# A state-space scan and a gated FFN on one core: compact pair states, decays of the first two blocks from TensorE, a shorter weight conversion, every engine in written order

## The chip, the core and the metric

The kernel runs on one core of a Trainium2 chip. A core has five engines with queues of their own: TensorE (PE; PEld are its weight loads), VectorE (DVE), ScalarE (ACT), GpSimd (POOL) and SyncE (SP), which here issues every DMA. The metric is the device time of one execution in microseconds, the median of several runs, less is better.

## What is computed

The first half is a Mamba-2 scan. Inputs are x (4 batches, 8 heads, 768 steps, 32 channels), a (one decay per step), B and C (16 states per step), all fp32. The second half is an FFN over the 4 x 768 = 3072 tokens, each with 8 x 32 = 256 channels, with 1536 hidden channels. Its three weight matrices come as fp64, the rest as fp32.

```
# per batch and head, in chunks of the sequence
cum  = cumsum(log(clip(a, 1e-6, 1)))
L    = exp(cum[i] - cum[j]) for i >= j, else 0
y    = (C B^T * L) x  +  exp(cum) * (C state)
state= exp(sum log a) * state + sum_j exp(cum[-1] - cum[j]) B[j] x[j]
# then per token
xn   = y / sqrt(mean(y*y) + 1e-6) * rms_g
out  = (silu(xn @ w_gate) * (xn @ w_val)) @ w_out
```

The result does not depend on the length of a chunk, and the kernel takes 128 steps.

## The kernel before

**Tiling.** A batch has 6 chunks of 128 steps, the run 24 chunks, or 12 pairs. Two pairs are the 512 tokens of one of 6 blocks. `load(p)` (line 80) brings x, B and C of a pair, time on the partitions, so that B and C come in runs of 64 bytes and x in runs of 128. All DMAs go through SP's queue.

**Decays.** The opening turns a into logs with time on the partitions, and by products with triangular matrices into the three factors of line 219. For the triangle L it also makes the cumulated logs as rows (line 229) and writes them to DRAM; `spread(g)` (line 279) reads the 8 x 128 values of a chunk back to all 128 partitions (512 KB written to SBUF), `decays(g)` (286) makes eight ScalarE exponentials with a bias per head, and `causal` clears the upper half on POOL (247).

**Scan of a pair.** `scale` multiplies B and C with their factors. `turn` (265) transposes B, scaled C and C of a chunk on TensorE; two ScalarE copies and one masked VectorE product take the result out of PSUM. `products` (295) forms C B^T for pairs of heads on 32-row strips of the array, and VectorE multiplies with L. `step_state` (313) multiplies scaled B with x as one 128 x 256 product per chunk, of which a mask keeps the blocks of equal heads, and carries the state on. `outputs` (337) adds the carried-in part (`inter`) and the part inside the chunk (`intra`, one 32-column matmul per head), copies y to SBUF on ScalarE and squares it on POOL. Norm: `norm_sums` and `norm_apply`.

**Weights.** VectorE turns fp64 words into fp32 in eight steps per piece of 512 columns (`convert`, lines 138 to 155); there are 18 pieces, in a ring of four raw buffers.

**FFN of a block.** `gate_val(blk, f)` (417) is four fp32 matmuls of 512 columns in two passes each for one of 12 hidden slices f, then sigmoid on ScalarE and two VectorE products, u and h. `project` (431) makes the output of 128 tokens from all 12. They share five PSUM banks with the scan's products.

**Order.** The kernel is written in the order below, with the next block's scan laid between the gate steps; a planner may start an instruction earlier or later than it is written, where its tiles allow it. In each step of the loop the scan of block blk + 1 runs beside the FFN of block blk, and L of block blk + 2 is made in the projection.

```
    for steps in scan_steps(0):
        run(steps)
    norm_sums(0)
    weights(2)
    norm_apply(0)
    for g in range(4, 8):
        decays(g)
```

Of the kernel before, what the change touches and what calls it, by code (L numbers as in the profile page):

```python
# [10 lines left out]
I32 = mybir.dt.int32  # L11
AF = mybir.ActivationFunctionType
# [5 lines left out]
def kernel(  # L18
# [27 lines left out]

    nc = tc.nc
# [11 lines left out]
    TB = 512  # L59
    NBLK = T // TB  # L60

# [3 lines left out]
    cvt = ctx.enter_context(tc.tile_pool(name="cvt", bufs=1))  # L65
# [3 lines left out]
    dram = ctx.enter_context(tc.tile_pool(name="dram", bufs=1, space=bass.MemoryType.DRAM))  # L69

# [3 lines left out]

    a_sb = const.tile([BH, S], FP32, name="a_sb")
    nc.sync.dma_start(out=a_sb, in_=a.rearrange("b h s -> (b h) s"))

    st = {}

    def load(p):  # L80
        b, c0 = divmod(2 * p, NC)
        xr = raw.tile([P, 2, NH, D], FP32, tag="xr", name="xr")
        br = raw.tile([P, 2, NH, N], FP32, tag="br", name="br")
        cr = raw.tile([P, 2, NH, N], FP32, tag="cr", name="cr")
        for i in range(2):
            sl = slice((c0 + i) * P, (c0 + i + 1) * P)
            for dst, src in ((br, B), (cr, C), (xr, x)):
                nc.sync.dma_start(out=dst[:, i], in_=src[b, :, sl, :].rearrange("h s n -> s h n"))  # L88
        st[p] = {"x": xr, "B": br, "C": cr}

    load(0)
    load(1)

    load(2)
    load(3)

    gcol = const.tile([P, 2], FP32, name="gcol")
    gv_ = moe_rms_g.rearrange("(q t d) -> q d t", t=2, d=D)
    for q in range(NQ):
        nc.sync.dma_start(out=gcol[q * D:(q + 1) * D, :], in_=gv_[q])  # L100


    WC = 256
    NWC = DF // WC
# [4 lines left out]
    def words(w):  # L109
# [4 lines left out]
    wsrc = {"g": words(moe_w_gate).rearrange("(q t d) f -> q d t f", t=2, d=D),  # L114
            "v": words(moe_w_val).rearrange("(q t d) f -> q d t f", t=2, d=D),
            "o": words(moe_w_out).rearrange("(o i) m -> i o m", i=P)}
    wraw = {}

    def fetch(name, j):
        r = raw.tile([P, 2, 2 * WC], I32, tag="wr", name="wr")  # L120
        if name == "o":
            nc.sync.dma_start(out=r, in_=wsrc[name][:, 2 * j:2 * j + 2])
        else:
            for q in range(NQ):
                nc.sync.dma_start(out=r[q * D:(q + 1) * D],
                                  in_=wsrc[name][q][:, :, 2 * WC * j:2 * WC * (j + 1)])
        wraw[name, j] = r.rearrange("p t (f w) -> p t f w", w=2)

    def convert(name, j):


        r = wraw.pop((name, j))
        lo, hi = r[:, :, :, 0], r[:, :, :, 1]
        cs = slice(WC * j, WC * (j + 1))
        dst = {"g": wg[:, :, cs], "v": wv[:, :, cs], "o": wo[:, 2 * j:2 * j + 2]}[name]
        shape = [P, 2, WC]
        e = cvt.tile(shape, I32, tag="e", name="e")
        nc.vector.tensor_scalar(out=e, in0=hi, scalar1=20, scalar2=0x7FF,
                                op0=ALU.logical_shift_right, op1=ALU.bitwise_and)
        nc.vector.tensor_scalar(out=e, in0=e, scalar1=896.0, scalar2=1151.0,  # L140
                                op0=ALU.max, op1=ALU.min)
        nc.vector.tensor_scalar(out=e, in0=e, scalar1=-896.0, scalar2=2.0 ** 23,
                                op0=ALU.add, op1=ALU.mult)
        nc.vector.scalar_tensor_tensor(out=e, in0=hi, scalar=-2 ** 31, in1=e,  # L144
                                       op0=ALU.bitwise_and, op1=ALU.bitwise_or)
# [12 lines left out]
    pending = [(n, j) for j in range(NWC) for n in "gv"] + [("o", j) for j in range(NWC)]  # L158
    AHEAD = 3
    for n, j in pending[:AHEAD]:  # L160
        fetch(n, j)

    def weights(k):
        for _ in range(min(k, len(pending))):
            if len(pending) > AHEAD:
                fetch(*pending[AHEAD])
            convert(*pending.pop(0))


    ident = const.tile([P, P], FP32, name="ident")  # L170
    make_identity(nc, ident)
    ones = const.tile([P, P], FP32, name="ones")
    nc.vector.memset(ones, 1.0)
# [10 lines left out]
    mean1 = const.tile([P, 1], FP32, name="mean1")  # L184
    nc.vector.memset(mean1, 1.0 / DM)
# [339 lines left out]
```

## Time and profile before

| | |
|---|---|
| time, median of 3 runs | 535.24 us (534.09 to 536.27) |
| the profiled execution | 536.25 us, its span 534.5 us |
| TensorE busy | 481.3 us, 90% of the span |
| VectorE busy | 252.8 us, 47% |
| ScalarE busy | 159.7 us, 30% |
| POOL busy | 51.3 us, 10% |
| moved by DMA | 32.03 MB in 87868 packets |

The span is the time from the first to the last instruction in the trace; the device time holds a little more. A busy share is a mean over the span, and TensorE's 90% has stretches of half that in it, so the rows further down are read by stretch. PEclk is the granted TensorE clock, 1.00 for 2.4 GHz.

### The profile page before, as it was taken

The page shows a single profiled execution, that of the slowest core. Times are in us where ns is not written, and L with a number is a line of the kernel's source. Part 1 is how long each engine was busy: PE and PEld are TensorE (multiplying, and loading weights), DVE is VectorE, ACT ScalarE, POOL GpSimd, SP SyncE. Part 2 cuts the span into 40 slices and gives each one's busy share as a digit, 9 for nine tenths or more (in the row PEclk, how much of TensorE's full clock was granted, in tenths as well). Part 3 has the DMA queues.
Part 4 walks back from the last instruction along what each step waited for, and adds up shares of the span by engine and source line. Part 5 has one row for each costly group of instructions (what it writes and reads, how often), then busy time and mean ns, then how long its engine had stood idle before and what let it go on. Part 6 is the DMA issues. An engine that isn't in the chain of part 4 may idle for free.

```text
span 534.5 us, 5748 instructions
## 1 busy us (share of the span) xinstructions
PE 481.3 (90%) x2082; PEld 293.8 (55%) x2082; DVE 252.8 (47%) x503; ACT 159.7 (30%) x377; POOL 51.3 (10%) x53
## 2 busy tenths in 40 slices
PE   4519595878899999999999999999999999999997
PEld 3306343333587444785444784455864547844476
DVE  2484858877995535113645213555026561134410
ACT  3146578401454128502155303211011211011100
POOL 1013403000241001200001200000000001000000
PEclk9755697887979999999998999999999999999999
DMA  8899960222971023300250200000000000000000
GB/s 103 145 262 200 207 162 15 64 95 68 240 160 49 0 66 53 109 21 10 20 115 5 70 20 11 0 1 0 21 20 1 1 1 10 21 10 0 1 10 29
DMA packets 87868, 32.03 MB, mean 60 GB/s; under 512 B 76864, under 2 KB 80128, under 8 KB 87840
## 3 DMA queue, kind: packets, MB, share of 16 engines
q1 hardware_dynamic: 87840, 31.67, 25.9%
q8 instruction: 16, 0.26, 0.2%
q14 instruction: 12, 0.10, 0.1%
HBM read 28.41 MB, written 3.24 MB: 59 GB/s over the span
## 4 chain that ended last, share of the span: by engine, by line
PE 74%; DVE 6%; ACT 5%; DMA 5%; SPq 4%; issue 4%; POOL 1%; DVEq 0%; POOLq 0%; ACTq 0%
PE o L434 24%; PE val L422 21%; PE gate L422 21%; DMA L<-rows 3%; SPq L88 3%; PE g L302 2%; ACT L L291 2%; PE y L354 2%; PE y L344 1%; PE ms L391 1%; PE rb L406 1%; ACT L425 1%; ACT L291 1%; DVE e L144 1%; POOL L L247 1%
## 5 line engine op out<-in xcount | busy, mean ns | idle before, releaser
L422 PE MATMUL val<-xn,wv 128*128 128x512 f32 x288 | 140.4, 611 | 7.8 <-DVE wv L155 7.1
L422 PE MATMUL gate<-xn,wg 128*128 128x512 f32 x288 | 142.2, 617 | 0.9 <-DVE xn L409 0.9
L434 PE MATMUL o<-wo,h 128*128 128x256 f32 x576 | 130.6, 386 | 1.1 <-DVE h L429 1.1
L434 PEld LDWEIGHTS o<-wo,h 128*128 128x128 f32 x576 | 110.6, 194 | 18.5 <-issue 2.4
L427 DVE TENSOR_TENSOR u<-sg,gate 128x512 f32<-128x512 f32 x72 | 49.4, 686 | 118.9 <-ACT sg L425 118.8
L422 PEld LDWEIGHTS val<-xn,wv 128*128 128x128 f32 x288 | 55.7, 195 | 78.7 <-issue 65.8
L425 ACT ACTIVATE sg<-gate 128x512 f32<-128x512 f32 x72 | 43.0, 597 | 153.7 <-PE gate L422 150.8
L422 PEld LDWEIGHTS gate<-xn,wg 128*128 128x128 f32 x288 | 54.5, 198 | 58.2 <-issue 50.3
L291 ACT ACTIVATE L<-L,neg 128x128 f32<-128x128 f32 x192 | 58.3, 389 | 20.4 <-DMA L<-rows 20.3
L429 DVE TENSOR_TENSOR h<-u,val 128x512 f32<-128x512 f32 x72 | 49.4, 687 | 29.4 <-PE val L422 29.0
L437 ACT COPY ob<-o 128x256 f32<-128x256 f32 x24 | 8.9, 372 | 109.1 <-PE o L434 108.1
L378 POOL TENSOR_TENSOR sq<-yt 128x512 f32<-128x512 f32 x12 | 15.1, 1258 | 264.2 <-ACT yt L377 264.2
L247 POOL TENSOR_SCALAR_AFFINE_SELECT L<-L 128x1024 f32<-128x1024 f32 x24 | 28.0, 1168 | 112.4 <-ACT L L291 107.6
L309 DVE TENSOR_TENSOR L<-g,L 128x256 f32<-128x256 f32 x96 | 33.4, 417 | 6.0 <-PE g L302 3.2
L354 PE MATMUL y<-L,xr 128*32 128x128 f32 x384 | 17.9, 300 | 17.3 <-DVE L L309 17.3
L409 DVE SCALAR_TENSOR_TENSOR xn<-yt,gcol,rb 128x512 f32<-128x512 f32 x12 | 8.5, 744 | 39.1 <-PE rb L406 39.0
L354 PEld LDWEIGHTS y<-L,xr 128*32 128x32 f32 x384 | 11.8, 117 | 25.1 <-DVE L L309 19.5
L302 PE MATMUL g<-CT,BT 32*128 32x256 f32 x192 | 21.0, 470 | 3.2 <-DVE u L427 3.2
L302 PEld LDWEIGHTS g<-CT,BT 32*128 32x128 f32 x192 | 11.7, 214 | 14.9 <-issue 8.7
L377 ACT COPY yt<-y 128x512 f32<-128x512 f32 x12 | 7.0, 585 | 40.6 <-PE y L344 40.6
L271 ACT COPY BT<-tp 128x128 f32<-128x128 f32 x24 | 6.3, 263 | 39.8 <-PE tp L269 31.4
L320 PE MATMUL A_ps<-xr,Bd 128*128 128x256 f32 x40 | 12.9, 406 | 3.7 <-DMA xr<-in_x_dram 2.9
(72 smaller groups left out, 293.4 us busy)
## 6 DMA issues: line engine op xcount, KB each, us to landing
L<-rows SPq DMA_DIRECT2D x24, 512.0 KB, 5.7
xr<-in_x_dram SPq DMA_DIRECT2D x24, 128.0 KB, 3.4
wr<-in_moe_w_gate_dram SPq DMA_DIRECT2D x24, 128.0 KB, 3.8
wr<-in_moe_w_val_dram SPq DMA_DIRECT2D x24, 128.0 KB, 3.6
wr<-in_moe_w_out_dram SPq DMA_DIRECT2D x6, 512.0 KB, 3.6
out_dram<-ob SPq DMA_DIRECT2D x24, 128.0 KB, 1.7
br<-in_B_dram SPq DMA_DIRECT2D x24, 64.0 KB, 3.0
cr<-in_C_dram SPq DMA_DIRECT2D x24, 64.0 KB, 2.9
```

The source lines that it names most:

```text
L88: nc.sync.dma_start(out=dst[:, i], in_=src[b, :, sl, :].rearrange("h s n -> s h n"))
L247: nc.gpsimd.affine_select(out=out_, in_=in_, pattern=[[0, NH], [1, P]], compare_op=ALU.is_ge, fill=0.0, base=0, channel_multiplier=-1)
L291: nc.scalar.activation(out=L[:, h], in_=L[:, h], func=AF.Exp, bias=neg[:, c, k:k + 1])
L302: nc.tensor.matmul(out=g[q][:, i], lhsT=s["BT"][r, i], rhs=s["CT"][r, i], start=(i == 0), stop=True, tile_position=(32 * q, 0), skip_group ...
L309: nc.vector.tensor_tensor(out=L, in0=g[q][:, i], in1=L, op=ALU.mult)
L354: nc.tensor.matmul(out=y[32 * q:32 * q + 32, t, i], lhsT=s["x"][:, i, 2 * q + t], rhs=Ls[2 * p + i][:, 2 * q + t], start=not opened and i ...
L378: nc.gpsimd.tensor_tensor(out=sqs[blk][:, :, tk], in0=yts[blk][:, :, tk], in1=yts[blk][:, :, tk], op=ALU.mult)
L422: nc.tensor.matmul(out=dst, lhsT=w[:, t, fs], rhs=xns[blk][:, t], start=(t == 0), stop=(t == 1))
L425: nc.scalar.activation(out=sg, in_=g, func=AF.Sigmoid)
L427: nc.vector.tensor_tensor(out=u, in0=sg, in1=g, op=ALU.mult)
L429: nc.vector.tensor_tensor(out=h, in0=u, in1=v, op=ALU.mult)
L434: nc.tensor.matmul(out=o, lhsT=hs_[blk, f][:, k * P:(k + 1) * P], rhs=wo[:, f], start=(f == 0), stop=(f == NF - 1))
```

## The change

- *Written order.* The planner is switched off: every engine takes its instructions in the order of the program. SP does so too.
- *Triangle decays.* For the first two blocks (chunks 0 to 7) L no longer goes by DRAM. `spans(g)` spreads the logs of a chunk over 128 columns and clears them below the diagonal on POOL, `sums(g)` multiplies with a triangular matrix on TensorE (two PSUM banks per chunk) and takes the exponential of 512 columns at a time on ScalarE, `select(g)` clears the upper half. For chunks 8 to 23 the spread sums by DRAM stay; `spread` is issued in gate steps 8 and 11, `decays` and `select` in the projection.
- *Conversion.* Eight VectorE steps become five; two clamps become ScalarE `Relu` steps. A piece is begun in one call of `convert` and finished in the next. There are 11 pieces, seven of them 1024 columns wide, in a ring of three raw buffers, one DMA each.
- *Pair states.* The states keep only the blocks of equal heads: `states(p)` makes four matmuls of 64 columns per chunk on column strips of the array, and `inter` four matmuls on quarter arrays where two full ones were. C is loaded twice as halves of even and odd heads into buffers that hold zeros for the others, so that the masked product of `turn` goes; `turn` makes four transposes and one ScalarE copy of all. The pair's products with L are four VectorE steps of 512 columns where eight of 256 were.
- *Smaller things.* The norm's factors are spread by transposes (one pass) where matmuls with the identity took two. Fewer buffers: L for three pairs, 12 hidden tiles where there were 15, single yt and rsb.

```diff
-    cvt = ctx.enter_context(tc.tile_pool(name="cvt", bufs=1))
+    cvt = ctx.enter_context(tc.tile_pool(name="cvt", bufs=2))
...
+    ctx.enter_context(tc.manual_schedule())
...
+    for k in range(4):
+        crs.append(const.tile([P, 2, 2, NH, N], FP32, name="cr%d" % k))
+        nc.vector.memset(crs[k], 0.0)
...
+        cr = crs[p % 4]
...
+            nc.sync.dma_start(out=br[:, i], in_=B[b, :, sl, :].rearrange("h s n -> s h n"))
+            for t in range(2):
+                nc.sync.dma_start(out=cr[:, i, t, t::2],
+                                  in_=C[b, t::2, sl, :].rearrange("h s n -> s h n"))
...
+    pieces = [(n, c, w) for c, w in ((0, 256), (256, 512), (768, 512), (1280, 256)) for n in "gv"]
+    pieces += [("o", c, 4) for c in range(0, NF, 4)]
+    fetched, begun = [], []
...
+            r = raw.tile([P, shape[0], 2 * shape[1]], I32, tag="wr", name="wr", bufs=3)
+            nc.sync.dma_start(out=r, in_=src)
...
+        nc.vector.tensor_scalar(out=e, in0=hi, scalar1=0x7FF00000, scalar2=None,
+                                op0=ALU.bitwise_and)
+        ef = e.bitcast(FP32)
+        nc.scalar.activation(out=ef, in_=e, func=AF.Relu, scale=-8.0, bias=etop)
+        nc.scalar.activation(out=e, in_=ef, func=AF.Relu, scale=-1.0, bias=einf)
         m = cvt.tile(shape, I32, tag="m", name="m")
         nc.vector.tensor_scalar(out=m, in0=hi, scalar1=0xFFFFF, scalar2=0x100000,
                                 op0=ALU.bitwise_and, op1=ALU.bitwise_or)
-        l = cvt.tile(shape, I32, tag="l", name="l")
-        nc.vector.tensor_scalar(out=l, in0=lo, scalar1=8, scalar2=None,
-                                op0=ALU.logical_shift_right)
-        f = cvt.tile(shape, FP32, tag="f", name="f")
-        nc.vector.scalar_tensor_tensor(out=f, in0=l, scalar=2.0 ** -24, in1=m,
+        f = m.bitcast(FP32)
+        nc.vector.scalar_tensor_tensor(out=f, in0=lo.bitcast(U32), scalar=2.0 ** -32, in1=m,
                                        op0=ALU.mult, op1=ALU.add)
+        begun.append((hi, e, f, dst))
...
+    def finish():
+        hi, e, f, dst = begun.pop(0)
+        nc.vector.scalar_tensor_tensor(out=e, in0=hi, scalar=-2 ** 31, in1=e,
+                                       op0=ALU.bitwise_and, op1=ALU.bitwise_or)
         nc.vector.scalar_tensor_tensor(out=dst, in0=f, scalar=2.0 ** -20, in1=e.bitcast(FP32),
                                        op0=ALU.mult, op1=ALU.mult)
...
+    def convert():
+        if pieces:
+            fetch()
+        if fetched:
+            begin()
+        if len(begun) > 1 or (begun and not fetched):
+            finish()
...
+    load(0)
+    fetch(1)
+    load(1)
+    fetch(1)
+    gcol = const.tile([P, 2], FP32, name="gcol")
+    nc.sync.dma_start(out=gcol, in_=moe_rms_g.rearrange("(t p) -> p t", p=P))
+    fetch(2)
+    load(2)
+    load(3)
...
+    def spans(g):
+        b, c = divmod(g, NC)
+        lams[g] = ssd.tile([P, NH, P], FP32, tag="lam", name="lam")
+        causal(lams[g], la[:, c, b * NH:(b + 1) * NH].unsqueeze(2).to_broadcast([P, NH, P]))
+    def sums(g):
+        lam = lams.pop(g)
+        L = pair_tile(g)
+        for k in range(2):
+            hs = slice(4 * k, 4 * k + 4)
+            e = bank("e", (P, 4, P))
+            nc.tensor.matmul(out=e.rearrange("p h m -> p (h m)"), lhsT=after,
+                             rhs=lam[:, hs].rearrange("p h m -> p (h m)"),
+                             start=True, stop=True)
+            nc.scalar.activation(out=L[:, hs], in_=e, func=AF.Exp)
...
+    def select(g):
+        causal(pair_tile(g), pair_tile(g))
...
+        tp = mm.tile([P, 4, P], FP32, tag="tp", name="tp")
...
+        nc.scalar.copy(out=s["T"][:, i], in_=tp)
...
+            L = Ls[p][:, :, 2 * q:2 * q + 2].rearrange("p i t m -> p i (t m)")
+            nc.vector.tensor_tensor(out=L, in0=g[q], in1=L, op=ALU.mult)
...
+        A_ps = bank("A_ps", (P, 2, 2, D))
+        for i in range(n):
+            for q in range(NQ):
+                nc.tensor.matmul(
+                    out=A_ps[32 * q:32 * q + 32, i].rearrange("p t d -> p (t d)"),
+                    lhsT=s["Bd"][:, i, 2 * q:2 * q + 2].rearrange("p t n -> p (t n)"),
+                    rhs=s["x"][:, i, 2 * q:2 * q + 2].rearrange("p t d -> p (t d)"),
+                    start=(i == 0), stop=True, tile_position=(0, 32 * q),
+                    skip_group_check=True)
+        new = ssd.tile([P, 2, 2, D], FP32, tag="A", name="A")
+        nc.vector.tensor_tensor(
+            out=new[:, 0:n], in0=A_ps[:, 0:n],
+            in1=tmask.unsqueeze(1).unsqueeze(3).to_broadcast([P, n, 2, D]), op=ALU.mult)
...
+        y = mm.tile([P, 2, 512], FP32, tag="y", name="y")
...
+            S, CdT = state[2 * p + i - 1], s["T"][:, i, 1]
+            for q in range(NQ):
+                r = slice(32 * q, 32 * q + 32)
+                o = 64 * (q % 2)
                 nc.tensor.matmul(
-                    out=y[:, t, i],
-                    lhsT=state[2 * p + i - 1][:, t].rearrange("p q d -> p (q d)"),
-                    rhs=s["CdT"][:, i], start=not opened and i == 0 and t == 0, stop=True,
+                    out=y[o:o + 64, q // 2, i * P:(i + 1) * P],
+                    lhsT=S[r].rearrange("p t d -> p (t d)"), rhs=CdT[r],
+                    start=start, stop=True, tile_position=(32 * q, o),
...
-            nc.tensor.matmul(out=rb[:, k], lhsT=rsb[:, k], rhs=ident, start=True, stop=True)
+            nc.tensor.transpose(out=rb[:, k], in_=rsb[:, k], identity=ident)
...
+        hs_[blk, f] = h = ffn.tile([P, TB], FP32, tag="h", name="h", bufs=NF)
...
+    spans(0)
+    spans(1)
+    sums(0)
+    scale(0)
+    turn(0, 0)
+    turn(0, 1)
+    spans(2)
+    begin()
+    select(0)
+    sums(1)
...
+    spans(3)
+    select(1)
+    products(0)
+    states(0)
+    sums(2)
+    scale(1)
+    turn(1, 0)
+    turn(1, 1)
+    begin()
+    finish()
+    select(2)
+    sums(3)
+    outputs(0)
+    select(3)
+    products(1)
+    states(1)
+    convert()
+    spans(4)
+    spans(5)
+    outputs(1)
+    norm_sums(0)
+    sums(4)
+    convert()
+    norm_spread(0)
+    spans(6)
+    select(4)
+    sums(5)
+    norm_apply(0)
+    spans(7)
+    select(5)
+    sums(6)
+    select(6)
+    sums(7)
+    select(7)
...
+            [(states, p), (scale, q)],
...
-    for g in range(8):
-        spread(g)
-    for g in range(4):
-        decays(g)
...
             gate_val(blk, f)
+            if blk == 0:
+                convert()
             run(todo[f])
-            if blk == 0:
-                weights(2 if f % 2 == 0 and f < NF - 2 else 1)
-        for k in range(TB // P):
+            if blk + 2 < NBLK and f in (8, 11):
+                for g in range(4 * (blk + 2) + 2 * (f == 11), 4 * (blk + 2) + 2 * (f == 11) + 2):
+                    spread(g)
...
+                select(4 * (blk + 2) + k)
+            if blk + 1 < NBLK:
+                if k == 0:
+                    norm_sums(blk + 1)
+                if k == 1:
+                    norm_spread(blk + 1)
+                if k == 2:
+                    norm_apply(blk + 1)
```

## Rows read from the trace of the kernel before

**Rows 1.** stretches; columns: length, busy us (instructions) per engine, PEclk, DMA share, GB/s

```profile
0.00:63.60 63.60, 33.80 (x180) 22.75 (x180) 35.83 (x85) 27.34 (x83) 14.17 (x22) 0.68 0.89 179
63.60:146.80 83.20, 66.50 (x256) 32.79 (x256) 66.72 (x144) 34.36 (x76) 9.14 (x6) 0.85 0.43 114
146.80:170.00 23.20, 23.16 (x97) 19.93 (x98) 19.41 (x36) 10.62 (x35) 7.70 (x6) 0.87 0.52 115
170.00:243.00 73.00, 71.93 (x329) 43.95 (x328) 24.66 (x46) 27.43 (x58) 7.46 (x7) 1.00 0.20 47
243.00:321.60 78.60, 76.34 (x346) 46.80 (x345) 31.32 (x59) 26.48 (x56) 6.63 (x6) 0.98 0.20 41
321.60:469.35 147.75, 147.60 (x690) 91.47 (x689) 58.39 (x111) 24.41 (x53) 6.18 (x6) 1.00 0.02 8
469.35:534.50 65.15, 61.92 (x192) 36.13 (x191) 16.46 (x24) 9.03 (x17) 0.00 (x0) 1.00 0.03 10
```

**Rows 2.** chain of waits, opening; columns: start, us, what

```profile
63.56 3.78 PE gate L422 x4
```

**Rows 3.** timeline, opening; start, us, engine, line, operation, [idle before <-releaser]

```profile
7.07 0.33 ACT L217 ACTIVATE d_sb<-d_ps 128x192 f32<-128x192 f32 x1 [0.31 <-PE d_ps L214]
...
18.36 0.58 SPq L88 DMA_DIRECT2D xr<-in_x_dram  x1
...
34.00 9.46 ACT L291 ACTIVATE L<-L,neg 128x128 f32<-128x128 f32 x32 [12.47 <-DMA L<-rows]
```

**Rows 4.** DMA issues of the page; KB each, median us to landing

```profile
L<-rows SPq DMA_DIRECT2D x24, 512.0 KB, 5.7
...
wr<-in_moe_w_gate_dram SPq DMA_DIRECT2D x24, 128.0 KB, 3.8
```

**Rows 5.** timeline of VectorE, one quiet conversion piece

```profile
29.33 0.43 DVE L138 TENSOR_SCALAR e<-wr 128x512 int32<-128x512 int32 x1
29.68 0.42 DVE L147 TENSOR_SCALAR m<-wr 128x512 int32<-128x512 int32 x1
...
31.02 0.68 DVE L153 SCALAR_TENSOR_TENSOR f<-l,m 128x512 f32<-128x512 int32 x1
31.62 0.68 DVE L144 SCALAR_TENSOR_TENSOR e<-wr,e 128x512 int32<-128x512 int32 x1
...
33.06 0.43 DVE L138 TENSOR_SCALAR e<-wr 128x512 int32<-128x512 int32 x1
```

**Rows 6.** groups of instructions by line and shape; busy us, mean ns, idle before

```profile
L429 DVE TENSOR_TENSOR h<-u,val 128x512 f32<-128x512 f32 x72 | 49.4, 687 | 29.4 <-PE val L422 29.0
...
L425 ACT ACTIVATE sg<-gate 128x512 f32<-128x512 f32 x72 | 43.0, 597 | 153.7 <-PE gate L422 150.8 <-DVE e L140 2.8
...
L247 POOL TENSOR_SCALAR_AFFINE_SELECT L<-L 128x1024 f32<-128x1024 f32 x24 | 28.0, 1168 | 112.4 <-ACT L L291 107.6 <-DVE h L429 4.6
...
L153 DVE SCALAR_TENSOR_TENSOR f<-l,m 128x512 f32<-128x512 int32 x18 | 13.2, 734 | 0.0
```

**Rows 7.** timeline, a POOL select beside a conversion step

```profile
55.94 1.28 POOL L247 TENSOR_SCALAR_AFFINE_SELECT L<-L 128x1024 f32<-128x1024 f32 x1
...
56.19 1.31 DVE L147 TENSOR_SCALAR m<-wr 128x512 int32<-128x512 int32 x1
```

**Rows 8.** chain of waits, third block

```profile
258.49 1.91 PE gate L422 x4
260.40 1.72 PE val L422 x4
...
292.53 1.01 PE y L354 x32
...
298.21 5.18 PE o L434 x24
```

**Rows 9.** timeline, third block, where TensorE waits

```profile
275.65 1.28 ACT L291 ACT_TABLE_LOAD   x1 [1.47 <-DMA L<-rows]
...
281.81 1.21 PE L302 MATMUL g<-CT,BT 32*128 32x256 f32 x10 [2.15 <-DVE u L427]
```

More of the change, by code (lines that the diff above doesn't have):

```diff
@@ new lines, in states @@
+        new = ssd.tile([P, 2, 2, D], FP32, tag="A", name="A")
+        nc.vector.tensor_tensor(
+            out=new[:, 0:n], in0=A_ps[:, 0:n],
+            in1=tmask.unsqueeze(1).unsqueeze(3).to_broadcast([P, n, 2, D]), op=ALU.mult)
+        for i in range(n):
+            g, c = 2 * p + i, c0 + i
+            S = ssd.tile([P, 2, D], FP32, tag="S", name="S", bufs=6)
+            k = c * NB + b
+            if c == 0:
+                nc.vector.tensor_copy(out=S, in_=new[:, i])
+            else:
+                nc.vector.scalar_tensor_tensor(
+                    out=S, in0=state[g - 1], scalar=fcol[:, k:k + 1],
+                    in1=new[:, i], op0=ALU.mult, op1=ALU.add)
+            state[g] = S
@@ L348, in inter @@
                     skip_group_check=True)
-        def intra():
-            for i in range(2):
-                for t in range(2):
-                    for q in range(NQ):
-                        nc.tensor.matmul(
-                            out=y[32 * q:32 * q + 32, t, i], lhsT=s["x"][:, i, 2 * q + t],
-                            rhs=Ls[2 * p + i][:, 2 * q + t],
-                            start=not opened and i == 0 and t == 0, stop=True,
-                            tile_position=(0, 32 * q), skip_group_check=True)
@@ L439, in project @@
         nc.sync.dma_start(out=out[r0:r0 + P, :], in_=ob)
+    spans(0)
[8 more added lines that the diff above has]
+    sums(1)
+    fsel = const.tile([P, NC * NB, NH], FP32, name="fsel")
+    nc.vector.tensor_tensor(
+        out=fsel, in0=full.rearrange("p c (b h) -> p (c b) h", h=NH),
+        in1=hmask.unsqueeze(1).to_broadcast([P, NC * NB, NH]), op=ALU.mult)
+    fcol = const.tile([P, NC * NB], FP32, name="fcol")
+    nc.vector.reduce_sum(out=fcol, in_=fsel, axis=AX.X)
+    spans(3)
[32 more added lines that the diff above has]
+    select(7)
+    n_ps = bank("n_ps", (P, NC, BH))
+    nc.tensor.matmul(out=n_ps.rearrange("p c h -> p (c h)"), lhsT=mid, rhs=laf,
+                     start=True, stop=True)
+    neg = const.tile([P, NC, BH], FP32, name="neg")
+    nc.vector.tensor_scalar(out=neg, in0=n_ps, scalar1=-1.0, scalar2=None, op0=ALU.mult)
+    HR = NC * BH // 2
+    r_ps = bank("r_ps", (HR, 2, P))
+    for k in range(2):
+        nc.tensor.matmul(out=r_ps[:, k], lhsT=laf[:, k * HR:(k + 1) * HR],
+                         rhs=mid, start=True, stop=True)
+    r_sb = const.tile([HR, 2, P], FP32, name="r_sb")
+    nc.vector.tensor_copy(out=r_sb, in_=r_ps)
+    rows = dram.tile([2, HR, P], FP32, name="rows")
+    nc.sync.dma_start(out=rows.rearrange("k r m -> r k m"), in_=r_sb)
+    rowv = rows.rearrange("k r m -> (k r m)")
     def scan_steps(blk):
@@ L462, in run @@
             fn(*args)
-    for g in range(8):
-        spread(g)
-    for g in range(4):
-        decays(g)
-    for steps in scan_steps(0):
-        run(steps)
-    norm_sums(0)
-    weights(2)
-    norm_apply(0)
-    for g in range(4, 8):
-        decays(g)
     for blk in range(NBLK):
```

278 lines of the change are left out of this document (102 added, 176 removed).

## Prediction

> **What bounds the kernel now.** I read the stretches first, then the chain of waits, then the timeline of the stretches that lose time. The span falls into an opening of 63.6 us, a block 0 of 83.2 + 23.2 = 106.4 us, blocks 1 to 4 (73.0, 78.6 and 147.75 for two) and a block 5 with its tail of 65.15 [rows 1]. From 170 on TensorE is busy 98% or more, but for the third block and the tail, at a granted clock of 0.98 to 1.00: matmuls bound it. Before 170 they don't. In the opening TensorE is busy 33.8 of 63.6 us at a clock of 0.68. In the gate part of block 0 VectorE is busy 66.7 of 83.2 us.
>
> The opening's timeline and the chain show why: ScalarE sits idle for 12.47 us until the first spread DMA of decay exponents lands at 34.00, then works 9.46 us on the first four tiles [rows 3], and the first gate matmul starts at 63.56 [rows 2]. After that VectorE sets the pace: it converts fp64 words. In a quiet piece a single-source step starts 0.35 us before the next (29.33 to 29.68), the first combining step takes 0.60 (31.02 to 31.62), the other two 0.72 each (31.62 to 33.06), and the piece as a whole 3.73 (29.33 to 33.06) [rows 5]. All 18 such pieces [rows 6] are 67 us of VectorE.
>
> **Conversion.** Of eight VectorE steps per 512 columns five stay: two single-source (2 x 0.34), three combining (0.60 + 2 x 0.72), so 2.72 against 3.73, or 49 us for all. Most pieces are now 1024 wide. A step of 1024 is at most two of 512: 2.56 for the three steps of `begin` and 2.88 for the two of `finish`. I take a tenth off (2.35 and 2.6), since some of each start-to-start time won't grow with the columns, and 1.3 and 1.4 at 512. The two clamps go to ScalarE; the sigmoid of 512 columns takes 0.60 [rows 6], so two clamps of 1024 are about 2.1 us. They lie beside the VectorE steps that follow in the same `begin` and `finish` (some 4 us) and are needed one call later. If that cover is gone, each of the 11 pieces costs up to 2.1 us.
>
> **The opening.** The exponents for two blocks no longer come by DRAM. Per chunk there is one POOL select to spread (1.17, [rows 6]), four 512-column TensorE passes, two ScalarE exps of 512 (0.60 each by the sigmoid) and the old select. A pass of 512 columns takes 3.78/4 = 0.95 us at the low clock [rows 2] and 1.72/4 = 0.43 at the high one [rows 8], so a chunk is 1.7 to 3.8 us of TensorE; I take 2.6, since the clock was mixed here. The path, with steps from these rows:
> - 7.4: last decay factor (7.07 + 0.33, [rows 3]). The spreading select of chunk 0 needs only the logs and is ready.
> - Chunk 0 sums to 10, eight transposes of pair 0 to 11.5, chunk 1 sums to 14, exp to 15.2, select to 16.4. Pair 0's loads don't bind: 24 issues ended at 18.94, 0.74 each [rows 3], so eight end near 7 and the first weight piece, 3.8 us to land [rows 4], is there at 11.
> - Pair 0's products on VectorE, 4 x 0.69 less overlap, to 19; its states and pair 1's scaling, six small steps near 0.35 (a single-source start-to-start step, [rows 5]), to 21.
> - Sums of chunks 2 and 3, turns and clamps, output copy (0.60), square (taken as a select, 1.17) and select in written order to 28.5; pair 1's products to 31.1, states to 32.1.
> - Then the output copy stands behind piece 2's clamps on ScalarE: 0.6 + 2.1 + 0.6 to 35.4; square, sums of squares and root to 39.4. VectorE converts meanwhile (4.8) and gives way to POOL for 2.2, to 45.2. The norm's spread and transposes end at 46.
> - Sums of chunks 6 and 7 and three small products stand ahead of the gate on TensorE: 2 x 2.6 + 1.2 (896 columns, at 0.108 us per 128 as below, or twice that) and a little waiting, to 53.
> So the gate starts at 53 instead of 63.56. With all passes at the high clock I get 47, with all low and no overlap 63.
>
> POOL and VectorE get in each other's way: a conversion step that takes 0.42 when quiet took 1.31, starting at 56.19 while a select ran from 55.94 for 1.28 us [rows 7]. The change adds eight selects of 1.17, at most 9.4 us; the 2.2 above is what I place beside conversions. The Trainium skill, SBUF — State Buffer, section "SBUF: two separate sides", says that the two engines lock a shared port pair for the whole instruction and the loser blocks fully. This trace agrees (1.31 us), and by that rule taken in full (9.4 less 2.2) the opening would lose 7 us more, the first rival below.
>
> On SP the fourth weight fetch now waits for the first piece's `finish` (a ring of three), near 24 us, and the loads of pairs 2 and 3 stand behind it. They are first needed at 56, and 16 issues of 0.74 with landing end near 40: hidden. Without that slack of 16 us it would cost block 0 directly. The split of C into two DMAs makes 8 issues of 6 per pair: 2 x 0.74 x 12 = 18 us of SP over the whole run, which SP has to spare, since it feeds pairs two blocks ahead.
>
> **Block 0.** At 56 (one gate of 1.7 and a sigmoid of 0.6 after 53) VectorE has left the `finish` of piece 3 and both halves of pieces 4 to 10, one of each per gate step, so steps 0 to 7: begins 5 x 2.35 + 2 x 1.3 = 14.4, finishes 6 x 2.6 + 2 x 1.4 = 18.4. To it come eight u and h pairs at 2 x 0.60 (0.69 each, [rows 6], less the same overlap) = 9.6, the scan's products (4 x 0.6) and nine small steps near 0.3 = 5, and 2 for POOL. That is 49 us, against 8 x 3.44 = 27.5 (a gate and a val of 1.72, [rows 8]) plus about 6 us of TensorE in the same steps, so VectorE paces steps 0 to 7, to 105. The ring of weight buffers gives each 1 MB fetch one call, some 7 us; it needs about 6, by 3.8 for four of 128 KB and the rest at the rate of the opening (179 GB/s, [rows 1]). If it doesn't hold, each of three fetches adds 1 to 2 us.
> Steps 8 to 11 are then TensorE's: 4 x 3.44 and 3.3 of scan less the 3.5 it ran ahead = 13.5, to 118.5. The output projection is 4 x 5.18 [rows 8] plus 20 norm passes at 0.108, 2.2, to 141.5. (A block of 73.6 exceeds its 62 us of gates and projection by 11.6; less the norm that is the 6 + 3.3 of scan.) Before it was 170: 28.5 us less. Also gone here are the exponentials between sigmoids with their table loads of 1.28 us [rows 9].
>
> **Blocks 1 to 4.** TensorE's own work, per block: norm transposes 8 to 4 passes of 128 columns at 5.18/24/2 = 0.108 [rows 8], -0.43; turns 12 to 16 passes, +0.43; the state product from 6.7 passes of 256 (0.216) to 26.7 small ones, bounded by the narrow 128-column matmuls at 1.01/32 = 0.032 [rows 8] and by their own 64 columns alone, 0.054: -0.6 to 0, I take -0.6; the carried-in product from 13.3 passes of 128 to 26.7 on quarter arrays, 0.032 to 0.108 each: -0.6 to +1.4, I take 0. The first gate after the quarter-array products takes 1.91 instead of 1.72 [rows 8], 0.19 for the change of shape; the new states and carried-in products add four such changes per pair, 0 to 1.5 us per block, I take 0.75. The Trainium skill, TensorEngine Tiling (Array Packing), section "Key Properties", says that a change of tiling mode drains the engine. The trace's 0.19 us agrees with a drain at one such place, and by that rule at every place a block would be 0.75 us slower than I take. Sum: +0.15 on 73.6, the mean of the three blocks without a stall, so 73.7.
> The third block's extra 5 us go: there ScalarE loaded a table after a late spread at 275.65, and the next scan products waited 2.15 us for VectorE behind it [rows 9]. The spreads are now issued at gate steps 8 and 11 and used in the projection, 10 us later against 5.7 to land [rows 4]. Four blocks: 295, instead of 299.35. What is late next is TensorE itself. The shorter rings (decay tiles for three pairs, 12 hidden tiles, single norm buffers) cost nothing in written order: each slot's last reader stands a block half or more ahead of its next writer, or, for the hidden tiles, ends while the next block's first gate runs.
>
> **Sum.** 141.5 + 295 + 65.15 = 501.65 us of span. The profiled execution took 536.25 at a span of 534.5, 1.75 more, so 503.4; it lies 1.0 over the median of the runs shown (535.24), so 502.
>
> **Rivals.**
> - *The opening gains nothing* (0.15): the gate at 63, sums at the low clock, POOL and VectorE excluding each other in full. That is 7 us of POOL (9.4 less 2.2) and 3 of low clock. For it: the clock of 0.68 [rows 1]. Against: the sums keep TensorE busy where it idled. 512.
> - *Block 0 is better covered than I count* (0.12): gate at 47, VectorE 42 us in steps 0 to 7 because the wide steps cost less each. 502 - 6 - 6 = 490.
> - *The clamps bring table loads* (0.04), so the change does not relieve VectorE freely: two of 1.28 us at each of 11 pieces, those of the opening (4 x 2.56) on the path. Against it: copies stand between exps and sigmoids without a load in the timeline. 502 + 10 = 512.
> - *Program order stalls TensorE in every gate step* (0.05): with each engine held to the written order, a late VectorE or ScalarE entry holds the next gate's PSUM bank. Price w in each of the 60 steps; it decides from w = 33/60 = 0.55 us. At 0.65 it gives 541, slower. Against it: in a steady step TensorE needs 3.44 and the sigmoid, u and h together 1.97, with five banks as before.
> - My forecast has the rest, 0.64, with its own range 491 to 513.
>
> **Numbers.** About 0.5% is what a measurement of this kernel can tell from no change. The range for 8 in 10 runs from 485 to 520: the better case less 5 us, and the two cases at 512 plus 8 for wrong sizes. Faster 0.95, the same 0.01, slower 0.04 (the last rival, less the hundredth in which it just balances).
>
> **What would show it.** First gate at 53 (47 to 63); no spread DMA before the gate; conversions done by gate step 7, near 105; block 1's first gate near 141; blocks 1 to 4 equal, at 73 to 74.5. Wrong if VectorE idles in steps 0 to 7 for weight DMAs or sigmoids, or if any steady block shows gaps between gates.

## The result and the profile after

The changed kernel takes 501.98 us (median of 4 runs, 500.58 to 502.45) where the kernel before, run beside it, takes 534.66 (532.21 to 536.27): a ratio of 0.939 with an interval of 0.935 to 0.943. The profiled execution took 502.45 us at a span of 500.7.

The stretches of the kernel after, cut at the first gate, behind the last conversion step, and at the first gate of each later block, to within 0.3 us (columns as in [rows 1]):

```profile
0.00:49.85 49.85, 36.39 (x239) 21.20 (x240) 31.05 (x58) 23.38 (x37) 22.77 (x29) 0.90 0.68 150
49.85:102.80 52.95, 42.98 (x167) 19.16 (x165) 47.88 (x67) 22.59 (x29) 2.08 (x2) 0.93 0.52 141
102.80:142.80 40.00, 39.62 (x207) 28.34 (x208) 10.31 (x19) 11.90 (x32) 5.30 (x5) 0.92 0.03 11
142.80:216.20 73.40, 73.40 (x382) 44.06 (x381) 26.06 (x47) 24.21 (x56) 7.43 (x7) 1.00 0.25 51
216.20:289.30 73.10, 73.10 (x381) 43.94 (x381) 26.30 (x48) 24.21 (x56) 7.43 (x7) 1.00 0.24 51
...
362.40:435.50 73.10, 73.10 (x380) 43.85 (x379) 26.04 (x47) 15.78 (x31) 4.18 (x4) 1.00 0.02 8
435.50:500.70 65.20, 62.10 (x193) 36.29 (x191) 16.46 (x24) 9.03 (x17) 0.00 (x0) 1.00 0.03 11
```

Against [rows 1] the opening is 13.7 us shorter (49.85 for 63.56), block 0 13.4 (92.95 for 106.4), blocks 1 to 4 together 6.7 (292.7 for 299.35); the tail is the same. From 142.8 on TensorE is busy through each block. Ahead of that it waits: in the second stretch VectorE is busy 47.88 of 52.95 us and TensorE 42.98.

The chain of waits of the kernel after (start, us, what), block 0 and then the fourth block's scan, which answers to [rows 2, 8]:

```profile
49.85 1.72 PE gate L440 x4
...
73.78 3.71 PE gate L440 x4
...
105.26 3.71 PE gate L440 x4
...
308.62 0.25 PE A_ps L335 x8
308.87 1.91 PE gate L440 x4
...
330.34 0.36 PE A_ps L335 x16
330.70 1.91 PE gate L440 x4
...
335.35 0.38 PE y L370 x8
335.73 1.91 PE gate L440 x4
```

TensorE's timeline in block 0 (start, us, engine, line, operation, [idle before <-releaser]) shows what stood ahead of these gates, and one idle time of about the same length behind which nothing slowed:

```profile
59.34 0.33 PE L306 MATMUL tp<-ident,Cd 128*128 128x128 f32 x1 [2.51 <-DVE Cd L291]
...
59.72 1.88 PE L440 MATMUL gate<-xn,wg 128*128 128x512 f32 x4
...
71.71 2.07 PE L317 MATMUL g<-T 32*128 32x256 f32 x10 [2.47 <-DVE u L445]
...
103.19 2.07 PE L317 MATMUL g<-T 32*128 32x256 f32 x10 [2.30 <-DVE u L445]
```

Two readings. At 73.78 and at 105.26 a gate takes 3.71 us, which is the low of TensorE's two clock levels (1.2 GHz), and both follow products for which TensorE had stood idle, waiting for VectorE. In the scan the state products are short (0.25 and 0.36), but the gate behind each pays 1.91 for 1.72.

The timeline of all engines: a conversion step beside a POOL select, the end of the opening, and one whole call of the conversion, 1024 wide, with the u and h behind it. It answers to [rows 5, 7]:

```profile
11.53 1.27 POOL L239 TENSOR_SCALAR_AFFINE_SELECT L<-L 128x1024 f32<-128x1024 f32 x1
...
11.78 1.31 DVE L160 TENSOR_SCALAR m<-wr 128x512 int32<-128x512 int32 x1
...
45.03 0.63 PE L424 MATMUL rb<-ident,rsb 128*128 128x128 f32 x4 [2.08 <-DVE rsb L417]
45.49 3.60 PE L263 MATMUL e<-lam,after 128*128 128x512 f32 x8
...
60.92 0.69 DVE L154 TENSOR_SCALAR e<-wr 128x1024 int32<-128x1024 int32 x1
61.52 0.69 DVE L160 TENSOR_SCALAR m<-wr 128x1024 int32<-128x1024 int32 x1
62.25 1.23 DVE L163 SCALAR_TENSOR_TENSOR m<-wr,m 128x1024 f32<-128x1024 uint32 x1
63.39 1.22 DVE L169 SCALAR_TENSOR_TENSOR e<-wr,e 128x1024 int32<-128x1024 int32 x1
64.64 1.23 DVE L171 SCALAR_TENSOR_TENSOR wg<-m,e 128x1024 f32<-128x1024 f32 x1
65.79 0.68 DVE L445 TENSOR_TENSOR u<-sg,gate 128x512 f32<-128x512 f32 x1
```

A call takes 65.79 - 60.92 = 4.87 us of VectorE for 1024 columns; the eight steps took 2 x 3.73 [rows 5].

Groups of the kernel after by line and shape (busy us, mean ns, idle before): the two clamps, and table loads:

```profile
L158 ACT ACTIVATE e<-e,einf 128x1024 int32<-128x1024 f32 x7 | 8.0, 1150 | 0.2
L157 ACT ACTIVATE e<-e,etop 128x1024 f32<-128x1024 int32 x7 | 8.0, 1149 | 22.3 <-DVE e L154 22.3
...
L443 ACT ACT_TABLE_LOAD x5 | 6.4, 1283 | 0.1
...
L279 ACT ACT_TABLE_LOAD x4 | 5.1, 1283 | 0.1
```

The clamps bring no load: these nine stand at sigmoids and at the exponentials of the decays, and the only two others, at 0.80 and 4.59 us, stand ahead of the first clamp, at the logarithm and the first exponential.

### The profile page after: what moved, and what is told of

It is laid out like the page before. It is cut to its first block, busy times and chain, and to the rows that moved or that the text cites. A ratio compares the mean times of both kernels' runs of the same rounds, so it can differ in the third digit from the quotient of the medians.

```text
span 500.7 us, 5896 instructions
## 1 busy us (share of the span) xinstructions
PE 473.8 (95%) x2314; PEld 280.7 (56%) x2314; DVE 210.1 (42%) x356; ACT 155.3 (31%) x313; POOL 56.6 (11%) x60
## 4 chain that ended last, share of the span: by engine, by line
PE 82%; DVE 7%; SPq 1%; DMA 0%; issue 0%; ACT 0%; DVEq 0%; ACTq 0%
PE o L452 25%; PE gate L440 24%; PE val L440 22%; PE g L317 3%; PE y L379 2%; PE ms L407 2%; PE tp L306 1%; DVE e L169 1%; PE y L370 1%; DVE m L163 1%; DVE wo L171 1%; DVE u L445 1%; DVE h L447 1%; PE e L263 1%; PE A_ps L335 1%; PE rb L424 1%
## 5 line engine op out<-in xcount | busy, mean ns | idle before, releaser
L440 PE MATMUL val<-xn,wv 128*128 128x512 f32 x288 | 136.1, 595 | 0.0
L452 PE MATMUL o<-wo,h 128*128 128x256 f32 x576 | 127.4, 380 | 0.0
L395 POOL TENSOR_TENSOR sq<-yt 128x512 f32<-128x512 f32 x12 | 12.6, 1052 | 244.2 <-ACT yt L394 244.2
L279 ACT ACTIVATE L<-L,neg 128x128 f32<-128x128 f32 x128 | 39.1, 390 | 0.0
L324 DVE TENSOR_TENSOR L<-g,L 128x512 f32<-128x512 f32 x48 | 29.8, 683 | 9.8 <-POOL L L239 5.8
L317 PE MATMUL g<-T 32*128 32x256 f32 x192 | 19.1, 434 | 5.4 <-DVE u L445 5.1
L308 ACT COPY T<-tp 128x512 f32<-128x512 f32 x24 | 14.0, 584 | 27.3 <-PE tp L306 27.3
L317 PEld LDWEIGHTS g<-T 32*128 32x128 f32 x192 | 11.0, 197 | 16.5 <-DVE u L445 12.4
L157 ACT ACTIVATE e<-e,etop 128x1024 f32<-128x1024 int32 (+1 forms) x11 | 10.9, 995 | 27.7 <-DVE e L154 27.7
L263 PE MATMUL e<-lam,after 128*128 128x512 f32 x32 | 18.2, 710 | 0.9 <-DVE L L324 0.9
L379 PE MATMUL y<-L,xr 128*32 128x128 f32 x384 | 14.4, 281 | 2.3 <-DVE L L324 2.3
```

The lines of the kernel that those rows point to most:

```text
L263: nc.tensor.matmul(out=e.rearrange("p h m -> p (h m)"), lhsT=after, rhs=lam[:, hs].rearrange("p h m -> p (h m)"), start=True, stop=True)
L279: nc.scalar.activation(out=L[:, h], in_=L[:, h], func=AF.Exp, bias=neg[:, c, k:k + 1])
L308: nc.scalar.copy(out=s["T"][:, i], in_=tp)
L317: nc.tensor.matmul(out=g[q][:, i], lhsT=s["T"][r, i, 0], rhs=s["T"][r, i, 2:4].rearrange("p t m -> p (t m)"), start=(i == 0), stop=True, t ...
L324: nc.vector.tensor_tensor(out=L, in0=g[q], in1=L, op=ALU.mult)
L379: nc.tensor.matmul(out=y[o:o + 32, h // 4, i * P:(i + 1) * P], lhsT=s["x"][:, i, h], rhs=Ls[p][:, i, h], start=start, stop=True, tile_posi ...
```

## The experiments

Each ratio is to the kernel before as it ran beside that row. Expectations are given as they stood before each run.

| kernel | median us | ratio to before, 95% interval |
|---|---|---|
| after | 501.98 | 0.939 (0.935 to 0.943) |
| before, in written order | 569.33 | 1.065 (1.059 to 1.071) |
| after, eight steps of conversion | 521.28 | 0.975 (0.971 to 0.980) |
| after, all decays by DRAM | 518.71 | 0.971 (0.967 to 0.975) |
| after, most of the conversion left out | 478.41 | 0.896 (0.891 to 0.900) |
| after, with the planner | 501.63 | 0.945 (0.939 to 0.951) |
| after, full states | 509.04 | 0.959 (0.955 to 0.963) |
| after, calls of convert spread | 498.02 | 0.936 (0.931 to 0.942) |
| after, conversion earlier | 498.48 | 0.939 (0.934 to 0.944) |
| the same, loads later | 491.64 | 0.922 (0.918 to 0.926) |
| the same, calls spread too | 491.92 | 0.923 (0.919 to 0.927) |

### The order alone, on the kernel before

```diff
+    ctx.enter_context(tc.manual_schedule())
```

> The kernel before with one line more: every engine held to the written order, nothing else changed. Theory (the gain is work taken off the opening and off VectorE, the order only keeps it in place): 525 to 545 us, no gain near the change's 33; the ScalarE table loads between sigmoids in block 0 go (6 to 8 us less there), but the gate starts later, since the exponentials of chunks 4 to 7 now stand whole ahead of the first sigmoid (10 us). Rival (the written order is what gained): 500 to 515 us.

Missed by far: 569.33 us. Its first gate starts at 80.43, block 0 takes 125.95, the later blocks 73.8 to 74.4, the third no more than the others. The timeline of ScalarE and VectorE in the opening shows why:

```profile
9.97 0.42 DVE L259 TENSOR_TENSOR Cd<-cr,d_sb 128x256 f32<-128x256 f32 x1
...
34.03 9.45 ACT L292 ACTIVATE L<-L,neg 128x128 f32<-128x128 f32 x32 [26.54 <-DMA L<-rows]
...
43.82 0.42 DVE L274 TENSOR_TENSOR CT<-tp,tmask 128x256 f32<-128x256 f32 x1 [33.44 <-ACT CdT L273]
```

ScalarE's copies stand behind the exponentials, which stand behind the spread DMAs, and VectorE waits 33.44 us for a copy with all its conversions behind that wait in order. The planner had put conversions there [rows 5]. The stall of the third block [rows 9], though, goes by the order alone.

### Eight steps again

```diff
-        nc.vector.tensor_scalar(out=e, in0=hi, scalar1=0x7FF00000, ...)
-        nc.scalar.activation(out=ef, in_=e, func=AF.Relu, scale=-8.0, bias=etop)
-        nc.scalar.activation(out=e, in_=ef, func=AF.Relu, scale=-1.0, bias=einf)
+        nc.vector.tensor_scalar(out=e, in0=hi, scalar1=20, scalar2=0x7FF, ...)
+        nc.vector.tensor_scalar(out=e, in0=e, scalar1=896.0, scalar2=1151.0, ...)
+        nc.vector.tensor_scalar(out=e, in0=e, scalar1=-896.0, scalar2=2.0 ** 23, ...)
...
+        nc.vector.tensor_scalar(out=lo, in0=lo, scalar1=8, ...)
```

> The kernel after, but with the eight VectorE steps of the old conversion (the two clamps back on VectorE, the shift of the low word back), pieces and order as after. Theory (VectorE paces gate steps 0 to 7): three more steps of 0.60 us per 1024 columns, 6.5 such pieces left at the gate = 12 us in block 0 and up to 4 in the opening: 512 to 518 us. Rival (the steps are paced by TensorE or by a wait for the next sigmoid): under 507.

521.28 us, 19.3 more than after, more than expected. The gate starts at 56.3 (+6.45, where up to 4 was expected), block 0 takes 105.53 (+12.6, about as expected). Its stretch of block 0:

```profile
56.30:161.83 105.53, 88.89 (x373) 50.09 (x373) 69.91 (x106) 21.38 (x47) 7.36 (x7) 0.85 0.27 75
```

VectorE is busy 69.91 us in all of block 0, where after has 47.88 + 10.31, and TensorE, idle longer, is granted 0.85. The other blocks are as in after. Of the three parts undone this one costs most.

### Decays by DRAM for the first chunks, too

```diff
-    spans(0)
-    spans(1)
-    sums(0)
+    for g in range(4):
+        spread(g)
...
+    for g in range(4, 8):
+        spread(g)
+    decays(0)
...
-    sums(1)
+    decays(1)
```

> The kernel after, but chunks 0 to 7 take their decays as the kernel before: rows to DRAM, spread DMAs, eight ScalarE exponentials each (L in four pair tiles for it); order otherwise as written. Theory (the DRAM trip and the eight small exponentials per chunk hold the opening): gate 6 to 10 us later than 49.85, 507 to 513 us. Rival (the old opening was late because its rows stood on SP behind loads and fetches): gate within 3 us, 500 to 505 us.

The edit also puts the later weight fetches and the loads of pairs 2 and 3 behind the first four spreads. 518.71 us, 16.7 more than after, over the expectation. ScalarE's timeline shows the first spread landing at 21.53 and the wait for it:

```profile
21.53 2.45 ACT L291 ACTIVATE L<-L,neg 128x128 f32<-128x128 f32 x8 [14.15 <-DMA L<-rows]
```

The gate starts at 62.91, 13.1 us later than after, and the gate of block 1 at 159.6, 16.8 later: in this written order the sums on TensorE are worth what the opening gained. How much of it the moved fetches and the order make isn't separated.

### Most of the conversion left out

From the third begun piece on one copying step stands for the steps, so this kernel leaves out the conversion of all later weights. (The expectation says the fifth; the trace shows two pieces converted.)

```diff
+        if len(pieces) < 7:
+            begun.append((hi, None, None, dst))
+            return
...
+        if e is None:
+            nc.vector.tensor_scalar(out=dst, in0=hi, scalar1=2.0 ** -34, ...)
+            return
```

> The kernel after with the conversion left out from the fifth begun piece on: one copying step per piece stands for its seven, so those weights are wrong and only the time counts. Theory (VectorE paces steps 0 to 7 and nothing else does): these steps fall from 53 us to TensorE's 34 to 37, and TensorE keeps its clock after them (3 us): 479 to 486 us. Rival (other waits of the written order hold these steps): above 490 us.

478.41 us, 0.6 below the range expected. The gate starts at 47.27, 2.6 us earlier than after, since two pieces of the opening are left out, too. Block 0 takes 73.00, and TensorE is busy in all of it:

```profile
47.27:120.27 73.00, 73.00 (x373) 43.84 (x373) 30.76 (x56) 21.38 (x47) 7.37 (x7) 1.00 0.39 108
```

So of after's 92.95 us in block 0 20 come with the conversion, TensorE's low clock among them, and the rest is a block like any other. Since TensorE is busy throughout, placing the conversion elsewhere cannot by itself bring block 0 under that.

### The planner on the kernel after

```diff
-    ctx.enter_context(tc.manual_schedule())
```

> The kernel after without its one line for the written order, so that the planner places the instructions as it did before. The kernel before lost 35 us by the written order (569.3 against 534.4), since VectorE's conversions then stood behind the opening's waits. Theory (the new program's order was written to keep VectorE fed and the table loads out, so it is part of the gain): 508 to 525 us. Rival (the work alone gives the gain, the planner fills VectorE as well): 495 to 504 us.

The theory fell: 501.63 us, 0.35 from after; the two ratios can't be told apart. Three stretches: the opening, the next 41.9 us, and block 1:

```profile
0.00:60.50 60.50, 40.91 (x243) 22.33 (x244) 40.06 (x69) 26.73 (x41) 24.43 (x29) 0.83 0.66 136
60.50:102.40 41.90, 39.52 (x174) 18.07 (x172) 41.33 (x65) 35.84 (x54) 7.80 (x4) 0.97 0.67 180
...
140.00:214.20 74.20, 74.04 (x382) 44.28 (x381) 25.87 (x47) 29.35 (x60) 7.46 (x7) 1.00 0.23 50
```

The planner moves conversions into the opening (VectorE busy 40.06 us of it, after 31.05), so the gate is 10.65 us later and block 0 13.45 shorter (79.5); block 1 then takes 74.2 for 73.4, and all that follows block 0 360.5 for 357.9. The two come out even, by other ways.

### Full states again

```diff
-            for q in range(NQ):
-                nc.tensor.matmul(out=A_ps[32 * q:32 * q + 32, i]..., tile_position=(0, 32 * q))
+            nc.tensor.matmul(out=A_ps[:, i]..., lhsT=s["Bd"][:, i]..., rhs=s["x"][:, i]...)
...
-            for q in range(NQ):
-                nc.tensor.matmul(out=y[o:o + 64, q // 2, ...], ..., tile_position=(32 * q, o))
+            for k in range(2):
+                nc.tensor.matmul(out=y[:, k, i * P:(i + 1) * P], ..., rhs=CdT)
```

> The kernel after with the pair states undone: one full-array state product of 256 columns per chunk, masked on VectorE, and two full carried-in products instead of four on quarter arrays; C and the transposes stay as after. Theory (small passes are cheaper, and a change of the array's shape costs about 0.19 us before the next gate): state products +0.9 us per block by 0.43 for 16 small passes against 0.86 for four of 256, less the changes of shape saved after them, 0.4: blocks of 73.4 to 74.0, 502.5 to 505 us. Rival (the changes of shape are what matters): blocks under 72.8, under 501 us.

509.04 us, 7.1 more than after, where 0.5 to 3 was expected. The chain of waits in its fourth block:

```profile
313.99 0.43 PE A_ps L334 x2
...
335.83 0.86 PE A_ps L334 x4
336.70 1.72 PE gate L433 x4
...
341.14 0.64 PE y L364 x4
341.78 1.72 PE gate L433 x4
```

Against after's rows the products are longer (0.43 and 0.86 for 0.25 and 0.36, 0.64 for 0.38) but the gates behind them are 1.72 again, so from first gate to first gate a block is only 0.5 to 0.8 us longer, about as expected. Most of the miss is the opening: the gate starts at 52.95, 3.1 us later. There VectorE's state steps are 256 wide (0.41 to 0.48 us each for 0.20 to 0.28), and the second pair's products on VectorE start at 29.54 where after has 27.87.

### Calls of convert spread over block 0

```diff
-            if blk == 0:
+            if blk == 0 and f % 3 != 2:
                 convert()
```

> The kernel after with the conversion calls of block 0 laid over gate steps 0, 1, 3, 4, 6, 7, 9, 10 instead of 0 to 7; nothing else moved. Theory (VectorE's work, some 58 us up to the projection, bounds block 0, and TensorE loses what it idles beside it and its clock after): first gate to projection 59 to 62 us instead of 70, 490 to 495 us. Rival (TensorE runs out of PSUM banks in every conversion step, wherever it stands): over 498 us.

498.02 us, short of the theory and by 0.02 in the rival's range; its ratio can't be told from after's. Of four executions one took 494.38, the others 497.97 to 498.22. The profiled one is the first; its span is 492.7, and its projection starts 61.9 us behind the first gate (49.91 to 111.79), as the theory said, where after's starts 70.0 behind it (49.85 to 119.86). TensorE's timeline, the second pair's products:

```profile
96.88 1.12 PE L317 MATMUL g<-T 32*128 32x256 f32 x10 [1.81 <-DVE u L445]
```

The products run at the high level here (1.12) and after's late ones did not (2.07). The other executions show spans of 496.3 to 496.5 and a mean clock of 0.972 to 0.973 for 0.986. One such group of products and the gate behind it cost after 2.7 us at the low level; that another makes most of the 3.6 to 3.8 us here is likely but not shown.

### Two more pieces in the opening

```diff
-    load(3)
...
     select(3)
+    convert()
+    load(3)
     products(1)
     states(1)
-    convert()
...
     outputs(1)
+    convert()
     norm_sums(0)
...
     norm_apply(0)
+    convert()
...
-            if blk == 0:
+            if blk == 0 and f in (0, 1, 2, 5, 7, 10):
                 convert()
```

> The kernel after with two changes of order: four conversion calls in the opening instead of two, placed where VectorE waits (before pair 1's products, after its outputs, and around the norm), with the loads of pair 3 behind the first of them; the six that are left in gate steps 0, 1, 2, 5, 7, 10. Theory (the conversion bounds block 0 and 20 us of it can be hidden: without it the block took 73 us): gate at 48 to 53, block 0 in 74 to 79 us, 482 to 490 us. Rival (the opening has no slack on VectorE, so the norm chain moves out by what is put in): gate after 56, 491 us or more.

498.48 us, a miss; the rival asked for a gate after 56 and doesn't hold either. The gate starts 2.9 us later (52.76), and block 0 gains 6.8 (86.15). The timeline of VectorE, TensorE and SP's queue shows what stood in the way:

```profile
54.24 0.40 SPq L103 DMA_DIRECT2D br<-in_B_dram  x1
...
64.25 9.71 SPq L139 DMA_DIRECT2D wr<-in_moe_w_out_dram  x3
...
70.41 0.69 DVE L154 TENSOR_SCALAR e<-wr 128x1024 int32<-128x1024 int32 x1 [3.23 <-DMA wr<-in_moe_w_out_dram]
...
75.21 2.07 PE L316 MATMUL g<-T 32*128 32x256 f32 x10 [5.26 <-DVE u L444]
77.21 3.78 PE L439 MATMUL gate<-xn,wg 128*128 128x512 f32 x4
```

The loads of pairs 4 and 5, which nothing needs before block 1, hold SP's queue from 54.24 to 64.15; the first of three fetches of output weights is issued at 64.25, VectorE waits 3.23 us for them, TensorE 5.26 behind VectorE, and the gate then runs at the low level.

### The same with these loads later

```diff
-        for p in (2 * blk + 4, 2 * blk + 5):
-            if p < NPAIR:
-                load(p)
+        if blk:
+            load_for(blk + 2)
...
             run(todo[f])
+            if blk == 0 and f == 2:
+                load_for(2)
```

> The early conversion with one edit: the loads of pairs 4 and 5, issued at the top of block 0, move behind gate step 2. Theory (SP's queue): in the early conversion the three output-weight fetches are issued at 64.25, behind ten us of loads (54.24 to 64.15), VectorE waits 3.2 us for the first, TensorE then 5.3 us for the scan's products, and the gate behind them runs at the low clock (3.71 instead of 1.72). With the loads behind, the first fetch goes out near 56, the 3.2 go, the idle stretch shrinks below 3 us and the clock stays: 492 to 495. Rival (VectorE's work alone sets block 0): the wait only moves to another place, 497 to 499 as before.

The theory held: 491.64 us, just under its range and 6.8 less than the run before it for the move of one group of issues. The same places in its timeline:

```profile
57.98 0.37 SPq L139 DMA_DIRECT2D wr<-in_moe_w_out_dram  x1
...
65.59 0.69 DVE L154 TENSOR_SCALAR e<-wr 128x1024 int32<-128x1024 int32 x1
...
70.39 1.13 PE L316 MATMUL g<-T 32*128 32x256 f32 x10 [1.95 <-DVE u L444]
71.44 1.98 PE L439 MATMUL gate<-xn,wg 128*128 128x512 f32 x4
```

The wait of VectorE is gone, TensorE's shrinks to 1.95, and the gate runs at the high level. Block 0 takes 80.1 us, 6.05 less than in the run before it and 12.9 less than after's, against the 73.0 without conversion. The 6.05 are these rows: 3.31 us less idle, 0.94 less for the products and 1.80 for the gate (3.71 to 1.91). Another 1.6 us lie in the opening (gate at 51.17), whose program is the same in both. In the run before, the eight passes for chunks 6 and 7 start 1.3 us later and take 5.29 us for 3.60, which is more time at the low clock; here TensorE waits 1.19 us for ScalarE, which takes part of that back. Why the two openings differ is not shown, and the next run, with this opening again, has its gate at 52.02.

### And the calls spread evenly

```diff
-            if blk == 0 and f in (0, 1, 2, 5, 7, 10):
+            if blk == 0 and f in (0, 2, 5, 7, 9, 11):
```

> The same, and the six calls of the conversion in block 0 stand at gate steps 0, 2, 5, 7, 9 and 11 instead of 0, 1, 2, 5, 7 and 10. Theory (both engines about even in block 0): TensorE needs 12 x 3.44 + 9.3 = 50.6 us there, VectorE 12 x 1.37 for u and h, 23.5 for the calls and 9 for the scan = 49; laid evenly the gate steps end some 55 us after a first gate at 52.8, so the projection starts near 108 where after has 119.85: 488 to 492. Rival (the order of the calls is of no account once the fetches come in time): within 1 us of the run before it.

The rival held: 491.92 us, no different. The theory's range holds this, too, but the projection starts at 107.90 where the run before it had 108.36 already. Block 0 is 1.3 us shorter (78.8) and the gate 0.85 later. So these two placings of the calls make no difference that can be told once the fetches come in time. The version with the loads later beats both kernels: 43.2 us less than before by these medians, of which after has 32.7.

## Why the prediction was right

It said 502 and 501.98 was measured. That it met the number so closely is luck: its steps were off by -3.2 us in the opening, +0.7 from the first gate to the last conversion step, +3.8 in the rest of block 0 and -2.3 in blocks 1 to 4, and these errors nearly cancel. The account of what bounds each stretch held, but for one step in block 0.

- *The opening, 53 predicted, 49.85 measured.* The path up to the norm came out as worked, each point within about a microsecond: its transposes ended at 45.7, predicted 46. The miss is the last term. I took 2.6 us for the sums of a chunk, 1.2 for three small products and a little waiting, 7 in all; the timeline shows 3.60 for the eight passes of both chunks, all at the high level, and 4.2 from the transposes to the gate. With two more pieces in the opening these passes took 5.29, so the 5.2 that I took is what they cost where the clock is low for part of them. The DRAM experiment shows that the sums are what makes this opening short.
- *POOL against VectorE.* The step at 11.78 took 1.31 us beside a select, as in [rows 7]; so did the norm's copy at 43.57 (0.43 at 131.39, with no select beside it). The rule of the Trainium skill (SBUF — State Buffer, section "SBUF: two separate sides") agrees with such pairs of instructions. But not every VectorE step beside a select is held up: the second pair's four products, which read PSUM, took 2.48 us beside two selects at 27.87 and 2.48 alone at 75.09. The 7 us that I drew from the rule for the opening did not come: VectorE idled there for 18.8 of 49.85 us, and the first gate came early.
- *Steps 0 to 7, 49 predicted, 50.3 measured* (from the first u, 52.24, to the end of the last conversion step, 102.54). VectorE paces them as said, and the conversion ends in gate step 7. A call costs 4.87 for the 4.95 that I took (2.35 + 2.6). The clamps are hidden beside it: 1.15 each, two per piece.
- *Steps 8 to 11 and the projection, 36.5 predicted, 40.3 measured* (102.54 to 142.80). The projection took 22.9 for 23.0; steps 8 to 11 took 17.3 for 13.5, at a granted clock of 0.81. Here the step failed: I let TensorE go on at the high clock behind a stretch that VectorE paces. The ten products at 103.19 took 2.07, where the runs with later loads and with spread calls show 1.13 and 1.12 for ten, and the gate behind them 3.71 for 1.91: 2.7 of the 3.8 us. Another 0.65 is TensorE's wait for the u of step 8, to 103.19, which I had left out.
- *Blocks 1 to 4, 295 predicted, 292.7 measured.* No block stalls. Of the terms, the changes of shape were right: six gates of 1.91 in a block, where full states leave two, are 4 x 0.19 = 0.76. The state products were taken too dear: 0.36 per 16 is 0.023 each, below the lower end that I had from 32-column matmuls, and the carried-in ones 0.38 per 8, 0.048 each: by 26.7 of each per block 0.6 and 1.3 us, where the old ones were 1.44 each by the prediction's prices. That is 0.4 us per block better than I took, of the 0.5 that a block came out shorter. That full states cost a block 0.5 to 0.8 bears it out.
- *The rivals.* The opening gained; no step of a steady block waits; no table load comes with the clamps. That program order itself would gain or lose was no part of my sum, and rightly: on the kernel after it makes no difference that can be told (501.63 against 501.98). On the kernel before it costs 35 us (569.33 against 534.39 beside it), so the order is only as good as the program that is written for it. The single parts undone (19.3, 16.7 and 7.1) add up to 43 against a gain of 32.7: they lean on each other, and how the whole divides among them stays open. The wider pieces, the halves of C with their transposes, and the norm's one-pass transposes were not undone singly.

## What to carry to other kernels

Where one engine paces a stretch that another will bound later, cost both: the work, and the clock at which the idle engine comes back. Before moving work earlier, follow its DMAs through the queue that issues them; here ten microseconds of loads that nothing needed yet cost 6.8 us, more than the place of the work itself. An order written by hand is judged with the waits of the program that it orders: the same switch cost 35 us on one version and nothing that can be told on the other.

## What the runs showed of the hardware

- TensorE fell to its low level behind short idle stretches in block 0, and the length of the last one doesn't tell whether it does. Ten products behind idle times of 2.30, 2.47 and 5.26 us took 2.07 us, those behind 1.81 and 1.95 took 1.12 and 1.13. Behind 2.19 us (calls spread) a val took 2.58 and the next gate 2.78, in between. But behind 2.51 us, at 59.34 in the kernel after, the next gate ran at the high level (59.72 to 61.44), and with the planner eight products behind 1.34 us took 2.07 and the gate behind them 3.71:

```profile
100.38 2.07 PE L316 MATMUL g<-T 32*128 32x256 f32 x8 [1.34 <-DVE u L444]
```

These are eight places and no rule.
- Sixteen state products of 64 columns on column strips take 0.36 us, 0.023 each, where their own columns at 0.108 us per 128 would make 0.054.
- A clamp of 1024 columns takes ScalarE 1.15 us, one of 512 0.72, where the sigmoid of 512 takes 0.60 [rows 6].
